# A softcap attention with two gated MLPs on one core: x's high part written by a second product from PSUM

## The chip, the cores and the metric

The kernel runs on one core of a Trainium2 chip. The metric is the device time of one execution in microseconds; the time before is the median of three runs. A profile of one further execution shows what each engine did: PE is TensorE (PEld its weight loads), DVE is VectorE, ACT is ScalarE, POOL is GpSimd and SP is SyncE, which issues most of the DMAs.

## The reference

The reference does attention with softcapped scores, then two MLPs, in float32 (cut):

```python
batch, n_heads, seq, head_dim = (4, 12, 448, 64)

scores = scale * np.matmul(q, k.transpose(0, 1, 3, 2))
scores = cap * np.tanh(scores / cap)
scores = scores - np.max(scores, axis=-1, keepdims=True)
attn = np.exp(scores)
attn = attn / (np.sum(attn, axis=-1, keepdims=True) + 1e-09)
x = np.matmul(attn, v)                     # then (B * S, H * D)

gate = 1.0 / (1.0 + np.exp(-(x @ w_gate)))  # d_ff 1536
x = gate * (x @ w_val) @ w_out
h = x @ w_in                               # d_ff 2048
return (h * np.cos(h)) @ w_out2
```

## The kernel before

The batch of four is done in two halves of two images. A half goes through attention, and its MLP follows. Attention works on pairs of heads: a half has 12 pairs (two images by six pairs of heads), so there are 24 in all. The transposed layout puts the two heads of a pair on the 128 partitions (64 each) and the 448 positions on the free axis.

The products need more than the rounded type of the fast matmul (fp32r), so an operand is kept as two parts: a high part, which is the value rounded to fp32r, and a low part, which is the value less the high part. For attention's result these are `x[:, 0]` and `x[:, 1]`, in a tile x of two images for each pair of heads. The first MLP reads them as its moving operands.

`attention(hf)` is a generator, and each `yield` ends a quarter of a step. In step i, with quarters c from 0 to 3, the work of several pairs stands side by side:

- `a_scores` of pair i: six matmuls into PSUM (L391) and a tanh on ACT (L394) in each quarter.
- `a_exp` (L400): exp on ACT over half of a pair's scores, and behind it on POOL the sum of the two blocks (L404). The first sum of pair i falls in c = 2, the second, which adds to it, in c = 0 of the next step.
- `a_sum` (L408, c = 2): DVE adds the last block to the sum of pair i - 1.
- `a_prep` (c = 0 and 2): PE transposes q, then k, of pair i + 2 into PSUM (t, L370); DVE rounds them (L374) and subtracts (L375) into st.
- `a_norm` of pair i - 2 (c = 0): two matmuls with ones make the denominators (den, L436); DVE takes the reciprocal (L439) and multiplies p.v by it (L440).
- `a_pv` of pair i - 1 (c = 2): 16 matmul passes into pv (L420).
- `a_split` of pair i - 2 (c = 2): DVE copies the product into x's high part (L448), and POOL subtracts it for the low part (L449). For the last pair of a half, DVE does the subtraction too.

The order in the code is the order on each engine (`tc.manual_schedule()`), each engine works through its queue in that order, and the waits are semaphores that follow from the data and from buffers that come free. The tiles t, pv and den share four PSUM buffers, the big tiles (st, p, x, g and others) share 18 SBUF buffers.

Beside attention of the first half runs the preparation of the first weight units: ACT takes absolute value and sign (L156, L158), DVE does four integer steps (L163, L165, L169, L173), then ACT rounds (L236) and POOL subtracts (L237). Three units are done in pieces between the quarters of the first stage. The second half's attention has no such pieces. In what follows the first attention stage is that of the first half, up to some 125 us, and the second one that of the second half, most of which stands at 390 to 485 us.

Of the kernel before, what the change touches and what calls it, by code (L numbers as in the profile page):

```python
# [8 lines left out]
F32R = mybir.dt.float32r  # L9
I32 = mybir.dt.int32  # L10
AF = mybir.ActivationFunctionType
ALU = mybir.AluOpType
PSUM = bass.MemoryType.PSUM

P = 128
# [12 lines left out]
def softcap_attention_gated_mlp_cos_mlp(  # L28
# [18 lines left out]
    nc = tc.nc  # L47
    B, H, S, D = q.shape
# [6 lines left out]
    BH = 2  # L55
# [39 lines left out]
    def big_tile(shape, dtype, name):  # L95
        return big.tile(shape, dtype, tag="big", name=name)
# [242 lines left out]
    x_t = {}  # L339
# [92 lines left out]
    def a_norm(b, hp):  # L432
        s = s_t.pop((b, hp))
        den = psA.tile([P, 512], F32, tag="A", name=f"den{b}_{hp}")
        for h in range(2):
            nc.tensor.matmul(den[h * D : (h + 1) * D, :S], lhsT=ones[:CP], rhs=s[:CP, h, :], start=True, stop=True)  # L436
        pv = pv_t.pop((b, hp))
        r = tmp.tile([P, 2, S], F32, tag="tmp", name=f"r{b}_{hp}")
        nc.vector.reciprocal(out=r[:, 0], in_=den[:, :S])  # L439
        nc.vector.tensor_tensor(out=r[:, 1], in0=pv[:, :S], in1=r[:, 0], op=ALU.mult)  # L440
        r_t[b, hp] = r

    def a_split(b, hp, engine):
        r = r_t.pop((b, hp))
        if b % BH == 0:
            x_t[hp] = big_tile([P, 2, BH, S], F32R, f"x{b}_{hp}")
        x = x_t[hp]
        nc.vector.tensor_copy(out=x[:, 0, b % BH], in_=r[:, 1])  # L448
        engine.tensor_tensor(  # L449
            out=x[:, 1, b % BH], in0=r[:, 1], in1=x[:, 0, b % BH].bitcast(F32), op=ALU.subtract  # L450
        )

    def attention(hf):
# [16 lines left out]
        for i in range(n + 1):  # L470
            if i + 3 < n:
                a_load(*mine[i + 3])
            for c in range(NC):
                if i + 1 < n and c == 3:
                    a_load_v(*mine[i + 1])
                if i < n:
                    a_scores(*mine[i], c)
                if i and c == 0:
                    a_exp(*mine[i - 1], 1)
                if i < n and c == 2:  # L480
                    a_exp(*mine[i], 0)
                if i and c == 2:
                    a_sum(*mine[i - 1])
                if i + 2 < n and c % 2 == 0:
                    a_prep(*mine[i + 2], c // 2)
                if 1 < i < n and c == NORM:
                    a_norm(*mine[i - 2])
                if i:
                    for cc in PVS[c]:
                        a_pv(*mine[i - 1], cc)  # L490
                if 1 < i < n and c == SPLIT:
                    a_split(*mine[i - 2], nc.gpsimd)
                if i >= n - 1 and c == 3:
                    a_norm(*mine[i - 1])
                if i == n and c == 0:
                    a_split(*mine[i - 2], nc.gpsimd)
                if hf == 0 and (i, c) in UNIT_LOADS:
                    w_load()
                if hf == 0 and (i, c) in UNIT_PIECES:
                    next(pieces, None)  # L500
                yield
        if hf == 0:
            for _ in pieces:
                pass
        a_split(*mine[n - 1], nc.vector)


# [270 lines left out]
```

## Time and profile before

| | |
|---|---|
| median of three runs | 1229.07 us (1226.44 to 1229.52) |
| profiled execution | 1222.13 us |
| its span, first to last instruction | 1220.3 us |
| PE busy | 1198.6 us, 98% |
| DVE busy | 685.8 us, 56% |
| ACT busy | 592.3 us, 49% |
| POOL busy | 443.3 us, 36% |
| DVE's copy into x (L448) | 24 times, 21.3 us in all |
| DVE's product (L440) | 24 times, 15.0 us in all |

Busy time is the sum of an engine's instructions, and it is an average over stages with different limits; the shares of a stage are read from the windows. An instruction that is held inside the engine counts as busy for as long as it is held. The chain of work that ended last tells which engine the end of the run depended on at each moment.

### The profile page before, as it was taken

The numbers are of one execution on the slowest core, as the hardware profiler recorded it, in microseconds if no ns is written. First come the engines' busy times: TensorE is split into PE (matmuls) and PEld (weight loads), VectorE is DVE, ScalarE is ACT, GpSimd is POOL, SyncE is SP. The second block draws the span as 40 slices with busy tenths as digits, with TensorE's granted clock in tenths as the row PEclk, the third lists the DMA queues.
The fourth block names the chain that finished last, engine by engine and source line by source line (L and its number), as shares of the span: only waits on it lengthen the run. The fifth ranks groups of instructions, "written<-read, shape, count | busy, mean of one in ns | idle before, by whom it ended". The sixth has DMA issues, their size and how long they took to land.

```text
span 1220.3 us, 15888 instructions
## 1 busy us (share of the span) xinstructions
PE 1198.6 (98%) x6342; PEld 1033.8 (85%) x6342; DVE 685.8 (56%) x729; ACT 592.3 (49%) x664; POOL 443.3 (36%) x234
## 2 busy tenths in 40 slices
PE   8989999999999999999999999999999999999998
PEld 4445889999987456999999998899999999999998
DVE  6998688778732997557566475501414434024242
ACT  6886455445426885444544345533515345344250
POOL 2767123233314675222233223432514333335140
PEclk9999999999999999999999999999999999999999
DMA  6431465555833340365655674221211631213003
GB/s 156 127 96 59 159 220 166 166 171 161 230 131 109 83 134 1 96 209 198 208 174 190 212 238 145 65 66 33 82 42 33 203 102 52 66 33 99 18 27 98
DMA packets 127082, 148.17 MB, mean 121 GB/s; under 512 B 50080, under 2 KB 100640, under 8 KB 127008
## 3 DMA queue, kind: packets, MB, share of 16 engines
q1 hardware_dynamic: 126720, 147.09, 39.4%
q8 instruction: 50, 0.82, 0.3%
q14 instruction: 24, 0.20, 0.0%
q10 hardware_dynamic: 288, 0.07, 0.0%
HBM read 112.13 MB, written 35.00 MB: 121 GB/s over the span
## 4 chain that ended last, share of the span: by engine, by line
PE 74%; DVE 13%; DMA 5%; ACT 4%; issue 3%; SPq 1%; POOL 0%; DVEq 0%; ACTq 0%; POOLq 0%
PE po L633 17%; PE ph L512 16%; PE pv L512 12%; PE pg L512 11%; PE py L512 7%; PE pv L420 4%; PE s L391 3%; DMA wz_raw<-in_moe_w_out_dram 2%; DVE r L439 2%; PE more L633 1%; DMA wi_raw<-in_moe_w_in_dram 1%; PE t L370 1%; DVE f L169 1%; DVE fb L169 1%; PE den L436 1%
## 5 line engine op out<-in xcount | busy, mean ns | idle before, releaser
L237 POOL TENSOR_TENSOR w<-f,w 128x768 fp32r<-128x768 f32 (+1 forms) x140 | 267.3, 1915 | 666.1 <-ACT w L236 570.2
L633 PE MATMUL po<-w,z 128*128 128x384 f32 x1248 | 220.8, 334 | 2.3 <-POOL w L237 2.3
L633 PEld LDWEIGHTS po<-w,z 128*128 128x128 f32 x1248 | 216.7, 188 | 3.2 <-POOL w L237 2.9
L512 PE MATMUL pv<-x,w 128*128 128x448 f32 x864 | 180.0, 366 | 1.0 <-DVE sg L561 1.0
L512 PE MATMUL pg<-x,w 128*128 128x448 f32 x864 | 179.8, 366 | 0.0
L512 PE MATMUL py<-g,w 128*128 128x448 f32 x864 | 177.5, 366 | 0.0
L512 PEld LDWEIGHTS pv<-x,w 128*128 128x128 f32 x864 | 162.0, 188 | 16.0 <-issue 3.1
L512 PEld LDWEIGHTS pg<-x,w 128*128 128x128 f32 x864 | 162.0, 188 | 14.6 <-issue 0.7
L512 PEld LDWEIGHTS py<-g,w 128*128 128x128 f32 x864 | 161.6, 188 | 13.7 <-issue 1.0
L236 ACT CAST w<-f 128x768 fp32r<-128x768 f32 (+1 forms) x140 | 112.1, 808 | 40.5 <-DVE f L173 16.2
L680 DVE TENSOR_SCALAR n<-u 128x896 f32<-128x896 f32 (+1 forms) x38 | 25.1, 660 | 186.6 <-ACT u L679 186.6
L512 PE MATMUL ph<-y,w 128*128 128x448 f32 x576 | 120.8, 371 | 2.3 <-ACT y L585 1.9
L512 PEld LDWEIGHTS ph<-y,w 128*128 128x128 f32 x576 | 109.2, 190 | 13.3 <-ACT y L585 2.2
L512 PE MATMUL ph<-ya,w 128*128 128x448 f32 x576 | 119.5, 368 | 0.0
L512 PEld LDWEIGHTS ph<-ya,w 128*128 128x128 f32 x576 | 108.1, 188 | 10.8
L394 ACT ACTIVATE p<-s,tanh_scale 112x896 f32<-112x896 f32 x96 | 93.1, 1011 | 42.6 <-PE s L391 42.5
L400 ACT ACTIVATE p<-p,cap_sb 112x1792 f32<-112x1792 f32 x48 | 86.3, 1799 | 0.1
L391 PEld LDWEIGHTS s<-st 64*112 64x112 f32 x576 | 45.7, 171 | 41.1 <-ACT p L394 19.0
L420 PE MATMUL pv<-p,v 112*64 112x448 f32 x384 | 77.5, 545 | 2.7 <-PE t L370 2.7
L439 DVE RECIPROCAL r<-den 128x448 f32<-128x448 f32 x24 | 70.8, 2950 | 8.6 <-PE den L436 8.6
L391 PE MATMUL s<-st 64*112 64x448 f32 x576 | 73.5, 381 | 1.6 <-ACT p L394 1.4
L404 POOL TENSOR_TENSOR sum<-p 112x896 f32<-112x896 f32 x24 | 55.8, 2327 | 48.7 <-ACT p L400 23.8
(82 smaller groups left out, 1206.3 us busy)
## 6 DMA issues: line engine op xcount, KB each, us to landing
f<-kept SPq DMA_DIRECT2D x96, 384.0 KB, 3.1
kept<-f SPq DMA_DIRECT2D x36, 384.0 KB, 2.7
wi_raw<-in_moe_w_in_dram SPq DMA_DIRECT2D x16, 768.0 KB, 5.7
kept<-fb SPq DMA_DIRECT2D x30, 384.0 KB, 2.7
wz_raw<-in_moe_w_out_dram SPq DMA_DIRECT2D x14, 768.0 KB, 5.1
wg_raw<-in_moe_w_gate_dram SPq DMA_DIRECT2D x12, 768.0 KB, 5.2
wv_raw<-in_moe_w_val_dram SPq DMA_DIRECT2D x12, 768.0 KB, 4.8
wo_raw<-in_moe_w_out_dram SPq DMA_DIRECT2D x12, 768.0 KB, 4.8
```

Source lines behind the costliest of these rows:

```text
L169: nc.vector.scalar_tensor_tensor(out=gi, in0=lo, scalar=28, in1=gi, op0=ALU.logical_shift_right, op1=ALU.bitwise_or)
L236: nc.scalar.copy(out=t[:, 0], in_=r)
L237: nc.gpsimd.tensor_tensor(out=t[:, 1], in0=r, in1=t[:, 0].bitcast(F32), op=ALU.subtract)
L391: nc.tensor.matmul(ps[:CP, h, :S], lhsT=st[r, ki, ks], rhs=st[r, qi], start=(n == 0), stop=(n == 2))
L394: nc.scalar.activation(out=pt[:CP, j], in_=ps[:CP, :, :S], func=AF.Tanh, scale=tanh_scale[:CP])
L400: nc.scalar.activation(out=pt[:CP], in_=pt[:CP], func=AF.Exp, scale=cap_sb[:CP])
L404: nc.gpsimd.tensor_tensor(out=s, in0=pt[:CP, 1] if half == 0 else s, in1=pt[:CP, 0], op=ALU.add)
L420: nc.tensor.matmul(pv[h * D : (h + 1) * D, :S], lhsT=tv[:, h, c, :], rhs=pt[:CP, j, h, :], start=(c == 0), stop=(c == NC - 1),)
L439: nc.vector.reciprocal(out=r[:, 0], in_=den[:, :S])
L512: nc.tensor.matmul(ps[:, c, :S], lhsT=w[:, wi, kk, :], rhs=x[:, xi, c, :], start=(first and (wi, xi) == (0, 0)), stop=(last and (wi, xi) = ...
L633: nc.tensor.matmul(pos_t[t][:, :NB], lhsT=zf[kk][:, zi, t * P : (t + 1) * P], rhs=ws[kk // UK][:, wi, kk % UK, :], start=(kk == 0 and (zi, ...
L680: nc.vector.tensor_scalar_add(out=n[:, c], in0=u[:, c], scalar1=ROUND)
```

## The change

The high part of x is no longer a copy of the finished product in SBUF. `a_norm` computes the product of pv and the reciprocal a second time, and this second product reads PSUM again and writes x's high part, rounded to fp32r. The first product, in float32, still goes to `r[:, 1]`; the subtraction for the low part reads both as before. The x tile is now allocated in `a_norm`, two quarters earlier.

```diff
         nc.vector.reciprocal(out=r[:, 0], in_=den[:, :S])
         nc.vector.tensor_tensor(out=r[:, 1], in0=pv[:, :S], in1=r[:, 0], op=ALU.mult)
+        if b % BH == 0:
+            x_t[hp] = big_tile([P, 2, BH, S], F32R, f"x{b}_{hp}")
+        nc.vector.tensor_tensor(out=x_t[hp][:, 0, b % BH], in0=pv[:, :S], in1=r[:, 0], op=ALU.mult)
         r_t[b, hp] = r
 
     def a_split(b, hp, engine):
         r = r_t.pop((b, hp))
-        if b % BH == 0:
-            x_t[hp] = big_tile([P, 2, BH, S], F32R, f"x{b}_{hp}")
         x = x_t[hp]
-        nc.vector.tensor_copy(out=x[:, 0, b % BH], in_=r[:, 1])
         engine.tensor_tensor(
```

On DVE the instruction moves. The place is the second step in which the first stage normalizes a pair (pair 1, the reciprocal at 33.73 us of the trace), with weight pieces between; r, pv and den are the tiles of that pair, st and t those of later pairs, f is a weight unit. Before:

```order
L439 RECIPROCAL r_1_476<-den_1_473 128x448
L440 TENSOR_TENSOR r_1_476<-pv_1_425,r_1_476 128x448
L163 TENSOR_SCALAR f_403<-f_403 128x768
L408 SCALAR_TENSOR_TENSOR sum_2_415<-sum_2_415,guard,p_2_1_405 112x896
L374 CAST st_5_465<-t_0_5_503 128x448
L375 TENSOR_TENSOR st_5_465<-t_0_5_503,st_5_465 128x448
L448 CAST x_1_519<-r_1_476 128x448
L165 TENSOR_SCALAR f_403<-f_403 128x768
```

Now:

```order
L439 RECIPROCAL r_1_476<-den_1_473 128x448
L440 TENSOR_TENSOR r_1_476<-pv_1_427,r_1_476 128x448
L443 TENSOR_TENSOR x_1_479<-pv_1_427,r_1_476 128x448
L163 TENSOR_SCALAR f_405<-f_405 128x768
L408 SCALAR_TENSOR_TENSOR sum_2_417<-sum_2_417,guard,p_2_1_407 112x896
L374 CAST st_5_465<-t_0_5_505 128x448
L375 TENSOR_TENSOR st_5_465<-t_0_5_505,st_5_465 128x448
L165 TENSOR_SCALAR f_405<-f_405 128x768
```

The write of x's high part moved ahead of L163 and L408, and L165 now follows directly on L375. In the next step (pair 2, the reciprocal at 42.66 us) another weight operation, L169, stands between the product and L408. Before:

```order
L440 TENSOR_TENSOR r_2_561<-pv_2_510,r_2_561 128x448
L169 SCALAR_TENSOR_TENSOR f_403<-wg_raw,f_403 128x768
L408 SCALAR_TENSOR_TENSOR sum_3_500<-sum_3_500,guard,p_3_1_490 112x896
L374 CAST st_0_550<-t_1_0_586 128x448
L375 TENSOR_TENSOR st_0_550<-t_1_0_586,st_0_550 128x448
L448 CAST x_2_602<-r_2_561 128x448
```

Now:

```order
L440 TENSOR_TENSOR r_2_561<-pv_2_512,r_2_561 128x448
L443 TENSOR_TENSOR x_2_564<-pv_2_512,r_2_561 128x448
L169 SCALAR_TENSOR_TENSOR f_405<-wg_raw,f_405 128x768
L408 SCALAR_TENSOR_TENSOR sum_3_502<-sum_3_502,guard,p_3_1_492 112x896
L374 CAST st_0_550<-t_1_0_588 128x448
L375 TENSOR_TENSOR st_0_550<-t_1_0_588,st_0_550 128x448
```

Here the new product stands ahead of L169 and L408. The orders of PE, ACT, POOL and SP are unchanged; on POOL the subtraction L449 still stands between the two sums L404.

## Rows read from the trace of the kernel before

**Rows 1.** Windows: stretch, its length, then busy time (and instructions) by engine

```profile
23.00:89.00 66.00, 59.45 (x386) 30.29 (x386) 64.96 (x67) 57.41 (x52) 43.06 (x23) 1.00 0.43 114
390.00:458.00 68.00, 68.00 (x446) 33.80 (x442) 63.35 (x65) 59.25 (x51) 44.74 (x24) 1.00 0.43 116
```

**Rows 2.** Waits of PE, 23 to 125 us: us in total, times, longest

```profile
PE den L436 <- DVE sum L408: 5.5, 5, 1.7
PE pv L420 <- PE t L370: 2.7, 4, 0.9
```

**Rows 3.** Chain that ended last, 10 to 135 us: start, us, what

```profile
30.53 2.10 DVE x L448
...
40.06 1.02 DVE x L448
...
46.27 2.35 DVE f L169
...
50.87 0.30 DVE x L448
...
59.01 1.03 DVE x L448
...
67.00 1.68 DVE x L448
...
73.86 1.93 DVE f L165
...
78.05 0.30 DVE x L448
```

**Rows 4.** Single lines: duration in ns as shortest/median/longest

```profile
L448 DVE CAST x<-r x24: 377/1104/2179, 30.4 to 484.4; 128x448 fp32r<-128x448 f32 x24
...
L440 DVE TENSOR_TENSOR r<-pv,r x24: 624/625/627, 27.6 to 483.7; 128x448 f32<-128x448 f32 x24
...
L375 DVE TENSOR_TENSOR st<-t,st x48: 624/624/626, 6.9 to 457.2; 128x448 fp32r<-128x448 f32 x48
```

**Rows 5.** Timeline, 22 to 50 us: start, us, engine, line, tiles, form

```profile
27.63 0.62 DVE L440 TENSOR_TENSOR r<-pv,r 128x448 f32<-128x448 f32 x1
...
28.18 1.15 DVE L408 SCALAR_TENSOR_TENSOR sum<-sum,guard,p 112x896 f32<-112x896 f32 x1
...
30.27 2.11 POOL L404 TENSOR_TENSOR sum<-p 112x896 f32<-112x896 f32 x1 [2.12 <-ACT p L400]
...
30.44 2.18 DVE L448 CAST x<-r 128x448 fp32r<-128x448 f32 x1
```

**Rows 6.** Timeline of POOL and of DVE, 383 to 390 us

```profile
384.10 4.50 POOL L237 TENSOR_TENSOR w<-f,w 128x768 fp32r<-128x768 f32 x2
...
384.17 2.72 DVE L408 SCALAR_TENSOR_TENSOR sum<-sum,guard,p 112x896 f32<-112x896 f32 x1 [3.17 <-POOL sum L404]
```

**Rows 7.** Timeline, 22 to 72 us, third and fourth step

```profile
45.68 2.12 POOL L404 TENSOR_TENSOR sum<-p 112x896 f32<-112x896 f32 x1 [1.07 <-issue]
...
54.07 1.78 ACT L400 ACTIVATE p<-p,cap_sb 112x1792 f32<-112x1792 f32 x1
...
56.67 1.14 DVE L408 SCALAR_TENSOR_TENSOR sum<-sum,guard,p 112x896 f32<-112x896 f32 x1
...
56.82 2.96 POOL L404 TENSOR_TENSOR sum<-p 112x896 f32<-112x896 f32 x1
...
58.43 0.97 PE L436 MATMUL den<-sum,ones 112*64 112x448 f32 x4
```

**Rows 8.** Timeline, end of the second stage

```profile
484.83 0.62 DVE L449 TENSOR_TENSOR x<-r,x 128x448 fp32r<-128x448 f32 x1
...
485.60 2.59 PE L512 MATMUL pg<-x,w 128*128 128x448 f32 x12
```

**Rows 9.** Timeline, inside the second stage

```profile
415.46 1.14 DVE L408 SCALAR_TENSOR_TENSOR sum<-sum,guard,p 112x896 f32<-112x896 f32 x1
...
416.37 2.21 POOL L404 TENSOR_TENSOR sum<-p 112x896 f32<-112x896 f32 x1 [1.36 <-issue]
```

## The prediction, as put down before the changed kernel was run

> **What bounds the kernel now.** I read the windows by stage first, then the waits of TensorE (PE), then the chain that ended last, then the timeline around the copy that goes. In the second attention stage PE is busy 68.00 of 68.00 us [rows 1]: nothing that VectorE (DVE) saves there can shorten the run. In the first stage, 23 to 89 us, it is the other way round: DVE is busy 64.96 of 66.00 us and PE 59.45 [rows 1]. PE's waits say for whom: 5.5 us for the sum of L408 and 2.7 us at pv [rows 2], where the matmul needs a bank that DVE's last read of t frees. Those 8.2 us are the most that any relief of DVE can give back. The chain of that stretch runs along DVE, and the copy that the change removes, L448, is on it six times [rows 3]. It is of one form each time and yet takes from 0.38 to 2.18 us [rows 4]. The timeline shows why: the copy at 30.44 starts while POOL's sum of 30.27 runs, and ends at 32.62, 0.24 us after that sum [rows 5]. So a copy in SBUF that meets a running POOL instruction waits for its end. The operations that convert weights show the same hold: L169 and L165 cost the chain 2.35 and 1.93 us at 46.27 and 73.86 [rows 3], and L408 at 384.17 took 2.72 us [rows 6] against 1.15 at 28.18 [rows 5]. The product L440, which reads PSUM and one operand in SBUF, never shows it: 624 to 627 ns in all 24 [rows 4].
>
> **The change, part by part.** *Removed:* the six copies on the chain, 2.10 + 1.02 + 0.30 + 1.03 + 1.68 + 0.30 = 6.43 us [rows 3]. The six later copies of this stage are not on the chain; I take nothing for them. *Added:* a second product of L440's form, right behind the first. L440 starts at 27.63 and L408 at 28.18 [rows 5], so it costs the chain 0.55 us; six make 3.30 us. Gross gain 6.43 - 3.30 = 3.1 us, if nothing else moves.
>
> Something else does: the holds do not belong to the copy. POOL's first sum of a pair starts when ACT's exp is done, whatever DVE does, and DVE's next operation that can be held meets it. Step by step, by pairs. Step 1 loses its 2.10 us copy, but PE runs without a gap there, so DVE only gains lead. In step 2 the copy's 1.02 us goes, and L165 right behind it now takes the rest of the hold; I keep 0.4 us. In step 3 the product stands ahead of L169, which was waiting for POOL anyway: the sum of 45.68 ends at 47.80 [rows 7] whatever DVE does, and L169 ends 0.8 us behind it, at 48.6 as before. That L169 absorbs the 0.55 us of the product, but also the 0.4 us won before; 0.3 us come back from the copy behind it. Step 6 (L165, 1.93 us [rows 3]) and step 7 (L173) are alike. In step 5 the hold of the fifth copy passes to L163 behind it, which leaves 0.2 us of its 1.68.
>
> Step 4 is where the change may lose. There L408 began at 56.67, just ahead of POOL's first sum at 56.82, which therefore took 2.96 us, not 2.11 as at 30.27 [rows 5, 7]. Exp ends at 54.07 + 1.78 = 55.85 [rows 7], and POOL's queue will be free by then, since its subtraction for x no longer waits for a late copy. L408 comes at 56.67 + 0.55 - 0.3 = 56.9 and finds the sum running until about 58.06. It then ends at 59.2 in place of 57.81, and den, which PE took up at 58.43 [rows 7], waits 0.8 us. Step 5 has no such loss and wins it back.
>
> What is left where PE takes over, at 89 us, is the little that steps 6 and 7 win behind their weight operations: **net gain 0.3 us**. As bounds I take 0.8 us lost (step 4 not won back) and 3.1 us won (no hold moves). The value lies near the lower end because three of the seven steps have a held weight operation that sets the time by POOL's end.
>
> *Moved and at no cost:* POOL's subtraction for x gets its input earlier (for the first pair at 28.8 in place of 32.62 [rows 5]) and stays behind the first sum in POOL's queue. Could it take its turn before a waiting DVE operation? At 384.17 L408 waited for the first of two POOL products and ran before the second (both took 4.50 us, so the second was pushed back) [rows 6]; I take it that DVE goes first. If not, a weight operation is held once more, a loss of the slower rival's kind. PSUM: pv is read 0.55 us longer; no wait row of PE names L440, so 0, and at most 0.55 us per pair if its bank were wanted at once. SBUF: x takes its buffer of 18 one allocation earlier; no DMA or queue of SP is moved. Second stage: PE covers it all. If that cover were gone, a pair's step on DVE would still be shorter, by the 1.1 us of the median copy [rows 4] less 0.55. At its end the last product is 0.62 us, the copy 0.40: x's low part would be ready 0.1 to 0.2 us later than 485.45, but PE's block of 485.60 [rows 8] first does six matmuls, about 1.2 us, on another x. So 0.
>
> **The rivals.** *Relief reaches PE.* For it: DVE's 98% in 23 to 89 us; against it: the holds that stay. It gives the gross 3.1 us, up to the 8.2 us of PE's waits: 1226.0 us, at the very best 1220.9.
>
> *L408 falls behind POOL's first sum in step after step* (slower). The product delays L408 by 0.55 us, POOL starts when exp ends, and whoever is later waits out the other. The point from which it decides is L408 starting after the sum. In the first stage that costs about 0.8 us of PE in step 4; if six of the seven steps met it and none was won back, 6 x 0.8 = 4.8 us, 1233.9 us. In the second stage L408 now leads by 0.91 us (415.46 against 416.37 [rows 9]); the product takes 0.55 of that, while the copy's absence lets the reciprocal start earlier, so it should stay ahead. Against the rival: weight operations hold DVE in only some steps, and a step without them is shorter than before. The Trainium skill (SBUF — State Buffer, "Who interferes with whom") says the port that DVE and GpSimd share is locked by whoever issues first, for the whole instruction, and that a DVE instruction with two SBUF inputs needs it. By that L408 can lose to the sum, as here; the trace agrees (2.72 us at 384.17).
>
> *The copy was the cheaper instruction* (slower, a little). A copy that nothing holds takes 0.38 us and the product 0.62 [rows 4]. If all holds stayed with the operations behind, each pair would pay 0.24 to 0.25 us more: 24 x 0.245 = 5.9 us of DVE, of which the six on the chain make 1.5 us: 1230.6 us. The Trainium skill (VectorE: DVE Perf Modes, "Mode 2×_2P — use both read ports for one tensor") has the rule behind this: a copy from SBUF to SBUF moves two elements a cycle, an operation with two tensors or a PSUM input one. The trace agrees with it for the shortest copies, and not for the median of 1.10 us, which a hold makes.
>
> *The change does nothing of the kind*: the product might take longer than L440 since it writes x's rounded type. L375 has the same types from PSUM at 624 to 626 ns [rows 4], so I give it little; at 1 us each it would cost 2.7 us on the chain.
>
> **How the numbers follow.** The profiled execution took 1222.13 us, span 1220.3; the median of the runs shown is 1229.07 (1226.44 to 1229.52), 0.6% above it. I carry the change over in microseconds: 1221.8 on the profile's scale, 1228.8 on the median's. Chances: forecast 0.62; relief 0.20; L408 behind 0.09; dearer product 0.07; nothing of the kind 0.02. About 0.3% (3.7 us) is what a measurement of this kernel can tell from no change. Faster by more needs the upper half of the relief, 0.10, plus the spread of the runs, 0.04: 0.14. Slower by more is most of the slower rival plus a little of the others: 0.08. Within: 0.78. The range, 1225.0 to 1231.5, takes in the forecast with the runs' spread of 3.1 us, the dearer product and the relief at 3.1 us; it leaves out the large relief and the worst of L408, under 0.2 together.
>
> **What would show it.** Right: no L448, 24 more products at 0.62 us; L169, L165 and L173 of the first stage end as late as before, with longer holds on L163 and L165; L408 near 57 us held by a sum; PE's wait at den still 5 us or more in 23 to 125 us; the second stage at 68 of 68 us. Wrong: den's wait falls to 3 us or less and the stage's end comes 2 us or more earlier (relief); L408 held in most steps (slower); product longer than 0.63 us.

## The result, and the profile after

The changed kernel took 1235.59 us (median of 6 runs, 1233.49 to 1239.51), the kernel before beside it 1229.30 (6 runs, 1225.02 to 1231.25): ratio 1.0071, interval 1.0052 to 1.0090. It is 6.3 us slower; the forecast was 1228.8 with a range up to 1231.5.

The profiled execution took 1233.49 us, its span 1231.7. By stage (stretch, its length, then busy time of PE, PEld, DVE, ACT and POOL, granted clock, DMA share, GB/s; first and last row answer to [rows 1]):

```profile
23.00:89.00 66.00, 59.57 (x364) 29.68 (x361) 64.68 (x62) 53.11 (x48) 41.30 (x22) 0.92 0.39 101
89.00:125.00 36.00, 31.76 (x180) 16.16 (x178) 32.34 (x28) 26.93 (x24) 26.00 (x15) 0.95 0.12 35
390.00:458.00 68.00, 68.00 (x439) 35.37 (x438) 57.25 (x61) 56.66 (x50) 45.88 (x25) 1.00 0.36 93
```

The second stage is as foreseen: DVE is relieved (57.25 in place of 63.35 us), PE is busy 68.00 of 68.00 us, and nothing comes of it. In the first stage PE's busy time has hardly moved (59.57 against 59.45), but with fewer matmuls in it (364 against 386) and at a granted clock of 0.92, where the row of before has 1.00. PE's waits of 23 to 125 us (us in total, times, longest), to be read beside [rows 2]:

```profile
PE den L436 <- DVE sum L408: 9.4, 5, 3.1
PE pv L420 <- PE t L370: 0.6, 1, 0.6
```

The wait for t has gone from 2.7 to 0.6, in part by DVE's relief (0.41 us at 42.84 is gone, 0.92 at 70.44 is 0.63). The other two, 0.69 each at 53.33 and 80.51, stand right behind den groups that came late, so PE itself came later there. The wait for L408 has grown by more, 5.5 to 9.4. The product itself is what was forecast, a little less (count, then shortest, median and longest in ns, beside [rows 4]):

```profile
L443 DVE TENSOR_TENSOR x<-pv,r x24: 614/614/616, 28.1 to 491.5; 128x448 fp32r<-128x448 f32 x24
```

**Where the time went** is read by taking the same group of matmuls in both traces and subtracting its start before from its start after. Before the loss begins PE is 0.58 us ahead (pv at 42.26 against 42.84). Then it falls behind in three bites: den at 50.51 against 49.73 is 0.78 late, and t behind it 2.67; den at 80.37 against 76.91 is 3.46 late; den at 92.42 against 86.45 is 5.97 late, and pv behind it 7.1. From there to 490 us little moves: den at 116.59 against 109.43 is 7.16 late. The first bite, in the timeline of the changed kernel, 44 to 62 us (start, us, engine, line, what, and in brackets the idle time ahead of it and its releaser):

```profile
45.40 0.61 DVE L443 TENSOR_TENSOR x<-pv,r 128x448 fp32r<-128x448 f32 x1
45.58 2.12 POOL L404 TENSOR_TENSOR sum<-p 112x896 f32<-112x896 f32 x1 [1.36 <-issue]
45.93 2.58 DVE L169 SCALAR_TENSOR_TENSOR f<-wg_raw,f 128x768 int32<-128x768 int32 x1
47.66 1.84 POOL L449 TENSOR_TENSOR x<-r,x 128x448 fp32r<-128x448 f32 x1
48.44 2.02 DVE L408 SCALAR_TENSOR_TENSOR sum<-sum,guard,p 112x896 f32<-112x896 f32 x1
50.51 1.76 PE L436 MATMUL den<-sum,ones 112*64 112x448 f32 x4 [3.09 <-DVE sum L408]
52.20 2.58 PE L391 MATMUL s<-st 64*112 64x448 f32 x12
...
58.15 2.10 POOL L404 TENSOR_TENSOR sum<-p 112x896 f32<-112x896 f32 x1 [0.82 <-POOL w L237]
58.37 2.83 DVE L408 SCALAR_TENSOR_TENSOR sum<-sum,guard,p 112x896 f32<-112x896 f32 x1
```

and the same place in the kernel before, with the den group of 109.43:

```profile
48.53 1.14 DVE L408 SCALAR_TENSOR_TENSOR sum<-sum,guard,p 112x896 f32<-112x896 f32 x1
49.73 0.97 PE L436 MATMUL den<-sum,ones 112*64 112x448 f32 x4 [1.72 <-DVE sum L408]
50.63 1.48 PE L391 MATMUL s<-st 64*112 64x448 f32 x12
51.25 1.78 POOL L449 TENSOR_TENSOR x<-r,x 128x448 fp32r<-128x448 f32 x1 [3.45 <-DVE x L448]
...
109.43 0.97 PE L436 MATMUL den<-sum,ones 112*64 112x448 f32 x4 [1.43 <-DVE sum L408]
```

Read the POOL rows. Before, L449 waited 3.45 us for the copy and ran long after L408. After, its input is written at 46.01 and it stands directly behind the sum. L169 had lain waiting since 45.93 and goes when the sum ends at 47.70, as forecast; L449, issued at 47.66, waits for L169 (1.84 us, where an undisturbed one takes 1.13). But when L169 ends, the waiting L449 goes before L408, which is next on DVE. L408 takes 2.02 us in place of 1.14, and den comes late. Then look at PE's own rows: the same den takes 1.76 in place of 0.97 us and s 2.58 in place of 1.48. The windows around the three waits (same columns as above) say why:

```profile
49.41:56.23 6.82, 5.72 (x22) 2.90 (x24) 6.75 (x7) 3.02 (x4) 3.16 (x3) 0.50 0.28 91
80.12:83.53 3.41, 3.16 (x12) 1.56 (x14) 3.38 (x5) 0.27 (x1) 2.08 (x1) 0.50 0.00 0
93.79:97.20 3.41, 3.41 (x16) 1.90 (x15) 3.38 (x3) 3.41 (x4) 2.38 (x2) 0.50 0.34 113
```

The granted clock was 0.50 there, the 1.2 GHz level. It fell within den's waits of 3.09 and 2.47 us, and 1.4 us behind the one of 2.53; the kernel before stood at 1.00, the 2.4 GHz level, in all of 23 to 125 us. The second bite is the first again, with L165 at 76.59, L449 at 77.91 and L408 held to 2.02 us at 78.29. The third is different: here POOL went twice running.

```profile
87.28 2.12 POOL L404 TENSOR_TENSOR sum<-p 112x896 f32<-112x896 f32 x1 [4.67 <-issue]
88.59 2.71 DVE L173 SCALAR_TENSOR_TENSOR f<-f,wv_raw 128x768 int32<-128x768 int32 x1
89.35 1.13 POOL L449 TENSOR_TENSOR x<-r,x 128x448 fp32r<-128x448 f32 x1
91.22 1.14 DVE L408 SCALAR_TENSOR_TENSOR sum<-sum,guard,p 112x896 f32<-112x896 f32 x1
92.42 0.97 PE L436 MATMUL den<-sum,ones 112*64 112x448 f32 x4 [2.53 <-DVE sum L408]
```

L173 waits out the sum and L449 too (2.71 us; 0.95 when free), and pushes L408 back.

**The working theory** (turn): L449, ready early, gets the port that both engines read through ahead of L408 or of the weight operation in front of it; PE's wait grows; and the half clock behind a long wait adds to it. The rivals are two: the 0.5 us of the product alone pushes L408 into POOL's sums (called position below), or the product is simply the dearer instruction, 0.61 us against 0.38 of a free copy (called dearer product).

### The profile page after: what moved, and what is told of

It is laid out like the page before. It is cut to its first block, busy times and chain, and to the rows that moved or that the text cites. A ratio compares the mean times of both kernels' runs of the same rounds, so it can differ in the third digit from the quotient of the medians.

```text
span 1231.7 us, 15887 instructions
## 1 busy us (share of the span) xinstructions
PE 1205.8 (98%) x6342; PEld 1034.9 (84%) x6342; DVE 690.6 (56%) x729; ACT 592.5 (48%) x664; POOL 442.6 (36%) x234
## 4 chain that ended last, share of the span: by engine, by line
PE 71%; DVE 14%; DMA 6%; ACT 5%; issue 3%; POOL 1%; SPq 1%; DVEq 0%; ACTq 0%; POOLq 0%
PE po L633 17%; PE ph L512 16%; PE pv L512 11%; PE pg L512 10%; PE py L512 7%; PE pv L420 4%; PE s L391 3%; DMA wz_raw<-in_moe_w_out_dram 2%; DMA wi_raw<-in_moe_w_in_dram 2%; DVE r L439 2%; DVE fb L163 1%; PE t L370 1%; PE more L633 1%; DVE fb L173 1%; DVE f L169 1%
## 5 line engine op out<-in xcount | busy, mean ns | idle before, releaser
L237 POOL TENSOR_TENSOR w<-f,w 128x768 fp32r<-128x768 f32 (+1 forms) x140 | 269.1, 1928 | 676.3 <-ACT w L236 591.7
L404 POOL TENSOR_TENSOR sum<-p 112x896 f32<-112x896 f32 x24 | 53.9, 2244 | 56.4 <-issue 25.3
```

Of the source, the lines that this page charges most:

```text
L237: nc.gpsimd.tensor_tensor(out=t[:, 1], in0=r, in1=t[:, 0].bitcast(F32), op=ALU.subtract)
L404: nc.gpsimd.tensor_tensor(out=s, in0=pt[:CP, 1] if half == 0 else s, in1=pt[:CP, 0], op=ALU.add)
```

## The experiments

The table gives, for every kernel run, how far PE is behind the first trace of the kernel before (us; median of up to five groups of matmuls from the mark on; the marks are times in that trace), and the ratio of times with its interval.

| kernel | 42 | 58 | 76 | 90 | 125 | ratio |
|---|---|---|---|---|---|---|
| changed kernel | -0.58 | 2.61 | 4.21 | 7.30 | 7.16 | 1.0071 (1.0052 to 1.0090) |
| after_again | -0.62 | 2.95 | 4.63 | 6.14 | 5.96 | 1.0063 (1.0039 to 1.0088) |
| before_again | 0.17 | 0.17 | 0.17 | 0.18 | 0.16 | 1.0021 (0.9997 to 1.0044) |
| only_pair_2 | 0.14 | 3.29 | 3.28 | 3.29 | 3.26 | 1.0012 (0.9995 to 1.0029) |
| not_2_5_6 | -0.59 | 0.38 | 0.38 | 0.41 | 0.06 | 1.0002 (0.9984 to 1.0019) |
| pair_2_low_late | 0.12 | 1.65 | 1.59 | 1.58 | 1.55 | one run |
| low_late_2_5_6 | -0.23 | 2.61 | 2.10 | 1.92 | 1.72 | 1.0025 (0.9998 to 1.0052) |
| low_behind_second_sum | 0.49 | 2.06 | 1.71 | 1.52 | 6.71 | 1.0058 (1.0031 to 1.0086) |
| only_pair_2_fill | -0.11 | 1.46 | 1.35 | 1.36 | 1.19 | one run |
| after_fill | -0.53 | 2.41 | 2.86 | 4.41 | 4.21 | 1.0044 (1.0017 to 1.0071) |
| not_2_5_6_fill | -0.46 | 0.96 | 0.44 | 0.47 | -0.01 | 1.0002 (0.9975 to 1.0029) |
| copy_at_norm | -0.41 | 3.05 | 5.63 | 6.74 | 11.78 | 1.0088 (1.0061 to 1.0114) |
| product_at_split | 0.64 | 0.95 | 1.98 | 4.59 | 4.82 | 1.0054 (1.0033 to 1.0076) |
| extra_product | 2.53 | 2.93 | 3.38 | 5.60 | 6.71 | 1.0160 (1.0137 to 1.0182) |
| sum_early_after | 0.88 | 4.07 | 3.47 | 6.52 | 8.71 | 1.0093 (1.0062 to 1.0124) |
| sum_early_before | 1.36 | 0.70 | -0.68 | 1.26 | 1.27 | 1.0023 (1.0005 to 1.0041) |
| pieces_late_after | 1.01 | 5.86 | 3.48 | 6.36 | 6.84 | 1.0055 (1.0035 to 1.0076) |

### What belongs to the change: both kernels once more

> The changed kernel once more, nothing altered. Theory turn (POOL's subtraction L449, now ready early and lying right behind POOL's first sum, takes the port that both engines read through between DVE's weight operation and L408; the end of L408 then comes late, PE waits for it with the den matmuls, and its granted clock halves behind the long waits): L408 is held by L449 again in the first attention stage (2.0 us in place of 1.14, at two or three of its steps), PE waits 8 to 10 us for L408 between 23 and 125 us, three stretches at half clock stand there, and PE is 6 to 8 us behind the kernel before at 125 us. Theory late part (the some 3 us that were lost between 490 and 560 us come with the execution and not with the change): PE loses under 1 us there this time. If they come with the change, 2.5 to 3.5 us again. Time 1233 to 1239.

> The kernel before once more, nothing altered, for a second trace of it. The profiled execution shown of it took 1222.13 us, under all of its other runs (1224.4 to 1231.3), and all four traces taken since lose 2.2 us against it between 490 and 600 us and about 1 us near 750 us. Theory late part (that comes with the execution): the new trace loses those 3 us too, from 490 us on, and is level with the first to within 1 us at 125 us; time 1226 to 1230. If the late part comes with the change, the new trace stays level from 490 to 600 us.

The two profiled executions of the changed kernel are 11.4 and 9.8 us longer than the first one of the kernel before. The second trace of the kernel before is level with the first up to 125 us (0.16), with the same waits for L408, and then loses 3.6 us by 490 and in all 13.5 us by the end, with nothing changed: its span was 1233.8. So differences behind 125 us come with the execution; the first trace of before was simply a quick one. The first 125 us repeat to some 0.2 us in the kernel before and to 1.2 in the changed one, and its delay there, 6.0 to 7.2 us, is as large as the 6.3 us by which the medians differ. It also repeats its rows: L408 takes 2.02 us at 48.40 and 2.01 at 78.66. One difference is the clock: the half stretch near 94 us was missing, and the third bite (76 to 90 us) is 1.5 us in place of 3.1. before_again's ratio shows what a timing here can't tell from 1.

### Which steps: the product for some pairs only

The two kernels are the kernel before with the second product for the pairs named, and the copy at its old place for the rest; x's tile is allocated in `a_norm` for all, as in the changed kernel. The diff is that of only_pair_2; not_2_5_6 has the condition `pairs.index((b, hp)) not in (2, 5, 6)`.

```diff
+        if pairs.index((b, hp)) == 2:
+            nc.vector.tensor_tensor(out=x_t[hp][:, 0, b % BH], in0=pv[:, :S], in1=r[:, 0], op=ALU.mult)
...
-        nc.vector.tensor_copy(out=x[:, 0, b % BH], in_=r[:, 1])
+        if not (pairs.index((b, hp)) == 2):
+            nc.vector.tensor_copy(out=x[:, 0, b % BH], in_=r[:, 1])
```

> The second product for one pair alone: the third of the 24 (index 2), whose reciprocal stands at 42 to 45 us. All others keep the copy at the old place. Up to 125 us two executions of the kernel before lay within 0.2 us of each other, so one step can be read from the trace. Theory turn: L449 of this pair runs right behind POOL's first sum, L408 takes 2.0 in place of 1.14, PE waits 3 us for it, half clock follows, and PE is 2 to 3.2 us behind the kernel before from 52 to 60 us; whatever of that DVE's later slack takes back, 1 to 3 us stay at 125 us: time 1229 to 1232. Theory sum of small delays (only all products together push L408 back): behind by 0.6 us at 52 us and by less than 1 at 125 us; 1227 to 1230.

> The second product for all pairs but three (indices 2, 5 and 6, at whose steps at 48, 78 and 88 us the changed kernel lost its time); these three keep the copy at the old place. Theory turn with its three steps: PE is within 1 us of the kernel before at 90 us, no half clock up to 90 us, at most 1.5 us behind at 125 us; time 1226 to 1230. Theory position (the place of the loss depends on where L408 stands against POOL's sums, and moves on): it turns up at other steps, 2 us or more at 90 us or 3 at 125 us, 1231 to 1235.

One product in 24 costs 3.3 us, and none of it is won back by 125 us: 3.29 at 58 us, 3.26 at 125. The other nine of the first stage together leave PE where it was (0.06 us; the kernel before repeated itself to 0.16). So the loss lies at the three steps, of which only that of pair 2 was tried by itself, and DVE's relief elsewhere (0.59 us at 42) comes to nothing by 125. not_2_5_6 also speaks against the dearer product: nine of the first stage's twelve products stand there in place of copies and cost nothing by 125 us. Against its expectation the clock halved at 49.41 us there too, with no product at that step: L169 went ahead of the first sum, which then held L408 to 2.98 us at 46.25. By the times only_pair_2 is 1.5 us slower, with an interval that includes the 3.3 us and none. In its timeline the first bite has the form of the third, since L169 comes 0.9 us later here:

```profile
45.80 2.12 POOL L404 TENSOR_TENSOR sum<-p 112x896 f32<-112x896 f32 x1 [1.06 <-issue]
46.85 2.97 DVE L169 SCALAR_TENSOR_TENSOR f<-wg_raw,f 128x768 int32<-128x768 int32 x1
47.88 1.13 POOL L452 TENSOR_TENSOR x<-r,x 128x448 fp32r<-128x448 f32 x1
49.74 1.14 DVE L408 SCALAR_TENSOR_TENSOR sum<-sum,guard,p 112x896 f32<-112x896 f32 x1
50.94 1.76 PE L436 MATMUL den<-sum,ones 112*64 112x448 f32 x4 [2.78 <-DVE sum L408]
52.63 2.58 PE L391 MATMUL s<-st 64*112 64x448 f32 x12
```

(The subtraction is L452 here.) The expectation's number, 2 to 3.2 us at 52 to 60, was met to 0.1 us; its detail, L408 itself held to 2.0 us, was not: L169 was.

### L449 out of the way

L449 is written behind POOL's second sum, one step later. So that no buffer is held longer, the first product then writes straight into the low part's place in the matmuls' type, which makes the low part zero.

```diff
-        nc.vector.tensor_tensor(out=r[:, 1], in0=pv[:, :S], in1=r[:, 0], op=ALU.mult)
+        low = x_t[hp][:, 1, b % BH] if pairs.index((b, hp)) in LATE else r[:, 1]
+        nc.vector.tensor_tensor(out=low, in0=pv[:, :S], in1=r[:, 0], op=ALU.mult)
...
-                if 1 < i < n and c == SPLIT:
+                if 1 < i < n and c == SPLIT and not (hf == 0 and i - 2 in LATE):
                     a_split(*mine[i - 2], nc.gpsimd)
...
                     a_exp(*mine[i], 0)
+                if hf == 0 and c == 0 and i - 3 in LATE:
+                    a_split(*mine[i - 3], nc.gpsimd)
```

This is low_late_2_5_6 (LATE = 2, 5, 6, on the changed kernel); pair_2_low_late does it for pair 2 on only_pair_2, low_behind_second_sum for all pairs of both stages.

> As the one before, and L449 of this one pair behind POOL's second sum instead of behind the first, written in place (the low part of this pair is zero by it). Theory turn: L408 takes 1.14 at 48 us, PE waits 1.5 to 2.2 us for it, no half clock near 50 us, PE is 0 to 0.7 us behind the kernel before from 52 to 60 us. Theory position: L408 starts 0.5 us later whatever L449 does, and PE is 1.5 us or more behind.

> The changed kernel with L449 of the three pairs 2, 5 and 6 written behind POOL's second sum, as in the run for one pair (their low part is zero by it, its time the same). Theory turn: L408 takes 1.14 at 48 and 78 us and the weight operation at 88 us is held by the sum alone (1.7 in place of 2.7); what stays is half clock at 50 us (1.0 to 1.6 us) and little else, so PE is 1 to 3 us behind at 125 us; time 1228 to 1232. Theory position (0.5 us later is enough without L449): 5 us or more behind at 125 us, 1233 to 1237.

> The changed kernel with L449 written behind POOL's second sum (one step later) in place of behind the first, so that it can't lie ready beside L408. To have no buffer held longer for it, the first product is written straight into the place of the low part, in the type of the matmuls, and L449 works in place: the low part is thereby zero, and its time the same. Theory turn: L408 takes 1.14 at the steps of some 48 and 78 us, PE waits 4 to 6.5 us for it in all, and the time is 1227 to 1231. Theory position alone (the product pushes L408 back until it meets POOL's next first sum, as at 58 us): that loss stays, one or two steps of 1 to 2 us each with their half clock behind them, 1230 to 1234. Theory dearer product: 1233 to 1237.

pair_2_low_late is the sharpest of these. Its timeline:

```profile
46.83 1.91 DVE L169 SCALAR_TENSOR_TENSOR f<-wg_raw,f 128x768 int32<-128x768 int32 x1
48.67 1.14 DVE L408 SCALAR_TENSOR_TENSOR sum<-sum,guard,p 112x896 f32<-112x896 f32 x1
49.86 1.35 PE L436 MATMUL den<-sum,ones 112*64 112x448 f32 x4 [1.75 <-DVE sum L408]
51.14 2.58 PE L391 MATMUL s<-st 64*112 64x448 f32 x12
```

The product is there, L449 is not: L169 absorbs the product's 0.55 us, L408 starts 0.14 us later than in the kernel before (48.67 against 48.53) and den 0.13. Theory position has lost for this step. Yet s takes 2.58 us, and PE is 1.6 us behind, which I had put at 0 to 0.7: the half clock came behind a wait of 1.75 us, after 1.72 had left it at full level in both traces of the kernel before.

With all three steps mended, 1.72 us of the 6.0 to 7.2 are left at 125 us. L408 took 1.14 us at the first two steps, and the third weight operation 1.23 in place of 2.71 (low_late_2_5_6, whose line numbers are one higher, so that L408 is L409 here and L173 is L174):

```profile
48.78 1.14 DVE L409 SCALAR_TENSOR_TENSOR sum<-sum,guard,p 112x896 f32<-112x896 f32 x1
...
61.27 0.97 PE L437 MATMUL den<-sum,ones 112*64 112x448 f32 x4 [1.50 <-DVE sum L409]
...
77.81 1.14 DVE L409 SCALAR_TENSOR_TENSOR sum<-sum,guard,p 112x896 f32<-112x896 f32 x1
...
86.17 1.23 DVE L174 SCALAR_TENSOR_TENSOR f<-f,wv_raw 128x768 int32<-128x768 int32 x1
```

**The turn, with the clock behind it, is 4.2 to 5.4 us of the loss.** This run has every product of the changed kernel, so the dearer product can have at most the rest, and half clock at 50 us and the prediction's step 4 (den at 61.27, of which more below) account for most of the 2.61 us at 58.

Moving L449 everywhere left PE 1.52 us behind at 90 us. L408 was clean at 48.79 and 86.93, but at 75.57 the first sum held it to 3.00 us, at no cost to PE (1.7 us behind ahead of it and after). Between 90 and 125 us it lost 5.2 us: there L408 was held at 102.09, 110.60 and 120.34 (2.04, 2.96 and 2.05 us), by L449 at its new place or by a sum, and the clock halved at 112 us. That expectation (1227 to 1231) missed; neither of L449's two places is clear of DVE in all steps.

### The clock by itself: matmuls of no use in the waits

In front of the den matmuls that wait, four more into the same bank (two in not_2_5_6_fill), overwritten by the true ones. The orders of DVE and POOL are left as they were.

```diff
+    FILL = {3: 4, 6: 4, 7: 4}
...
         den = psA.tile([P, 512], F32, tag="A", name=f"den{b}_{hp}")
+        k = pairs.index((b, hp))
+        for q in range(FILL.get(k, 0)):
+            pt = p_t[pairs[k + 1][0], pairs[k + 1][1], 0]
+            nc.tensor.matmul(
+                den[q % 2 * D : (q % 2 + 1) * D, :S], lhsT=ones[:CP], rhs=pt[:CP, 0, q % 2, :], start=True, stop=True
+            )
```

> The kernel with the second product for the third pair alone, and the same four matmuls of no use in front of the den matmuls that wait 2.8 us for L408 there. Theory clock: no half clock at 50 us, PE is 1.0 to 1.4 us behind from 52 to 125 us (L408's late end alone: den came 1.2 us later in that kernel) in place of 3.3. If the clock has no part: 3.0 to 3.6.

> The changed kernel with four matmuls of no use (2 x 448 columns twice, about 1.9 us by the den row of 0.97) in front of the den matmuls of three pairs, into the same bank, which the true ones then overwrite: PE works while it waits for L408 at the steps of 50, 80 and 92 us, where it waited 3.1, 2.5 and 2.5 us. DVE and POOL do the same as in the changed kernel. Theory clock (the half clock behind long waits is a loss of its own, about 3.9 of the 7.2 us at 125 us; the late L408 is the other 4.3): no half clock near 50, 80 and 93 us, and PE is 3 to 4.5 us behind the kernel before at 125 us instead of 6 to 7.2; time 1230 to 1233. If the late L408 is all: 6 to 8 us behind, 1234 to 1238.

> The kernel with the second product for all pairs but 2, 5 and 6, which was level with the kernel before at 125 us, having been 0.6 us ahead up to 47 us and lost 1.0 at a stretch of half clock at 49 us behind a wait of 1.9 us; two matmuls of no use (1.0 us) fill that wait. Theory clock: it stays 0.3 to 0.7 us ahead up to 125 us, and its time is 1225 to 1229, which no timing here can tell from the kernel before. If the clock has no part: level or behind at 125 us.

The first stage of after_fill, and its first bite:

```profile
23.00:89.00 66.00, 59.46 (x382) 29.42 (x381) 64.69 (x63) 53.80 (x48) 42.66 (x23) 1.00 0.38 100
```

```profile
47.41 1.72 PE L440 MATMUL den<-p,ones 112*64 112x448 f32 x8
50.55 0.97 PE L444 MATMUL den<-sum,ones 112*64 112x448 f32 x4 [1.43 <-DVE sum L408]
51.46 1.47 PE L391 MATMUL s<-st 64*112 64x448 f32 x12
...
58.44 2.57 DVE L408 SCALAR_TENSOR_TENSOR sum<-sum,guard,p 112x896 f32<-112x896 f32 x1
...
61.07 0.97 PE L444 MATMUL den<-sum,ones 112*64 112x448 f32 x4 [1.35 <-DVE sum L408]
```

L408 is held as before (2.02 us at 48.48), den starts at the same time as in the changed kernel (50.55 against 50.51), but den takes 0.97 and s 1.47 us: the clock stayed at 1.00 through 23 to 125 us. PE is 4.21 us behind at 125 instead of 5.96 and 7.16, and 1.19 instead of 3.26 where only pair 2 has the product (1.36 instead of 3.29 at 90). **The clock's share is 1.8 to 3.0 us**, less than the 3.9 I had expected, and 1.9 to 2.1 us of a single step's 3.3. One reason is in the last two rows. At 57.73 PE was 1.24 us late in place of 2.59, but then the first sum held L408 of 58.44, den waited 1.35 us, and PE was 2.4 us late again. So what the clock costs at the first bite hides what the next hold would cost, and the two can't be added. The third bite also took another form: L173 ran free at 88.06 (0.95 us), and L449 held L408 behind it (2.03 us at 88.93). The time, 1234.90, missed the 1230 to 1233 expected. By the times, 1.0044, it can't be told from the changed kernel, whose interval overlaps; the trace's 4.21 us would be 1.0034. not_2_5_6_fill missed in part: it stayed 0.3 us ahead past 52 us, but at 56.88 L408 then met a first sum that had begun at 56.49 (2.67 us), and the lead was gone by 58.

### The operation without the place, the place without the operation

```diff
# copy_at_norm, against the changed kernel
-        nc.vector.tensor_tensor(out=x_t[hp][:, 0, b % BH], in0=pv[:, :S], in1=r[:, 0], op=ALU.mult)
+        nc.vector.tensor_copy(out=x_t[hp][:, 0, b % BH], in_=r[:, 1])
# product_at_split, against the kernel before, in a_split
-        nc.vector.tensor_copy(out=x[:, 0, b % BH], in_=r[:, 1])
+        nc.vector.tensor_tensor(out=x[:, 0, b % BH], in0=pv[:, :S], in1=r[:, 0], op=ALU.mult)
# extra_product, against the kernel before, in a_norm
         nc.vector.tensor_tensor(out=r[:, 1], in0=pv[:, :S], in1=r[:, 0], op=ALU.mult)
+        nc.vector.tensor_tensor(out=r[:, 1], in0=pv[:, :S], in1=r[:, 0], op=ALU.mult)
```

> The copy from SBUF as in the kernel before, but written where the second product stands now, right behind the first product. Position without the product. Theory turn: L449 has its input as early as in the changed kernel and takes its turn ahead of L408, so L408 is held again at the steps of some 48 and 78 us, PE's waits for L408 are 8 us or more, and the time is 1232 to 1238. Theory dearer product (0.61 us of a product against 0.38 of a free copy, six times, on DVE's path): without the product there is nothing to lose, and the time is 1228 to 1230.

> The second product, but at the old place of the copy (behind L408 and one cast and product of L374 and L375). The operation without the position. A bank of PSUM is held longer by this, which may cost up to 0.5 us at a step. Theory turn: L449 gets its input some 4 us later, as in the kernel before, POOL stands idle when L408 starts, L408 takes 1.14 again at nearly all steps, PE waits 4 to 6.5 us for it, no half clock between 23 and 125 us, and the time is 1226 to 1231. Theory dearer product: 1232 to 1237, as in the changed kernel.

> The kernel before with its first product written twice, the copy from SBUF kept at its old place behind L408: the delay of the changed kernel (0.5 to 0.6 us in front of the weight operation and L408) without the early input of L449, and with the copy not taken away. The result is the same. Theory turn (L449 being ready early is what costs): L408 is not held by L449 in the first stage; the kernel loses what DVE's added work costs, up to 6 x 0.54 = 3.2 us, and not more: 1229 to 1232. Theory position (0.5 us later is enough for L408 to meet POOL's next sum, with PE's long waits and its clock halving behind them): L408 held by POOL's sums at 2 or more steps, PE's waits for it 8 us or more, half clock between 23 and 125 us, and 1233 to 1238.

copy_at_norm is slower than the product, 11.78 us behind at 125. L449 holds L408 at 48.84, 78.93 and 91.32 (2.02 us each) as in the changed kernel, with no product there, so the place by which L449 is released costs by itself. The run does not tell which instruction is dearer. The copy takes 0.39 us in the median, but at the three steps the first sum held it to 2.03 to 2.16 us, in place of the weight operation:

```profile
45.89 2.15 DVE L443 CAST x<-r 128x448 fp32r<-128x448 f32 x1
47.97 0.94 DVE L169 SCALAR_TENSOR_TENSOR f<-wg_raw,f 128x768 int32<-128x768 int32 x1
48.12 1.78 POOL L449 TENSOR_TENSOR x<-r,x 128x448 fp32r<-128x448 f32 x1 [0.33 <-DVE x L443]
48.84 2.02 DVE L408 SCALAR_TENSOR_TENSOR sum<-sum,guard,p 112x896 f32<-112x896 f32 x1
```

Against the dearer product stand not_2_5_6 and low_late_2_5_6.

product_at_split does not clear the old place: 4.82 us behind, outside what I expected of theory turn (1226 to 1231; it took 1233.6). L408 is clean (1.18 us and less), but another wait has come:

```profile
PE den L436 <- DVE st L375: 8.9, 5, 2.9
PE den L436 <- DVE sum L408: 1.5, 1, 1.5
```

The profile shows that den now waits for L375. My reading is that the late product holds pv's bank of PSUM longer, and that den then gets one of the four banks that L375 of a t frees last; the rotation itself was not traced. I had put this at 0.5 us a step, and because of it this run tells nothing on the turn.

extra_product (the delay, with L449 late and the copy kept) shows theory position at work where nothing absorbs it: L408 meets a first sum and is held to 2.5 to 3.1 us at 38.56, 58.99, 68.32, 96.69 and 105.82, and 6.71 us are lost at 125. Then it loses some 9.5 us more before 490: in the second stage L408 is behind the first sum in step after step (415.19, 424.98, 433.61 and so on, 1.85 to 3.04 us), where it led by 0.91 us before [rows 9].

```profile
L408 DVE SCALAR_TENSOR_TENSOR sum<-sum,guard,p x24: 1139/1854/3069, 21.0 to 492.5; 112x896 f32<-112x896 f32 x24
```

The median of L408 is 1854 ns here; it is 1144 in the changed kernel. At 18.6 us by the medians this is more than either theory had said (up to 1238), since I had not thought of the second stage. It has the copy and one product more, so it tells what a delay can do, not what the change does.

### Other orders

```diff
# sum_early_after and sum_early_before: L408 of the pair behind, right behind the reciprocal
         nc.vector.reciprocal(out=r[:, 0], in_=den[:, :S])
+        if then:
+            a_sum(*then)
# pieces_late_after
-    UNIT_PIECES = [(i, c) for i in range(2, BH * NP) for c in (1, 3)]
+    UNIT_PIECES = [(i, c) for i in range(2, BH * NP) for c in (2, 3)]
```

> The changed kernel with L408 written right behind the reciprocal, ahead of both products and of the weight operation; everything else stays. POOL's second sum, that L408 needs, ended at 44.2, 52.4 and so on, 0.6 to 2 us before the reciprocal's end, and POOL's next first sum starts 0.7 us or more behind that end. Theories turn and position alike say that the loss is L408's late end: with L408 1.1 to 3.6 us earlier it takes 1.14 at most steps, PE waits under 3 us for it between 23 and 125 us, no half clock stands there, PE is level with the kernel before or up to 4 us ahead at 125 us, and the time is 1224 to 1230. Theory dearer product (DVE's added work is the loss, wherever it stands): 1232 to 1237.

> The kernel before with the same move of L408 to right behind the reciprocal; the copy stays where it was, behind the weight operation. It tells what the move is worth by itself, and so whether the second product is a gain once L408 stands in front of it. If the product then gains its 0.5 us a step, this kernel is 1 to 3 us slower than the changed kernel with the move; theory dearer product: this one is quicker than it by 3 us or more. Time 1225 to 1231.

> The changed kernel with the first of the two weight operations of a step written one place later (c = 2 in place of 1), behind L408, so that nothing but the two products stands between the reciprocal and L408. Theory turn: at the steps of some 48 and 78 us it is now L408 that waits for POOL's first sum and goes as its turn comes, with L449 behind it and the weight operation behind that: L408 ends 0.5 to 1.5 us earlier than in the changed kernel, PE waits 4 to 6.5 us for it, and the time is 1227 to 1232. Theory dearer product: nothing changes, 1233 to 1237. If L408 meets the first sums in more steps than before, 1234 or more.

The time of sum_early_before lay where it was expected (1228.8), as slow as the kernel before or slower; the two with the product missed, pieces_late_after by little (1232.25 against 1232 at most). They all shorten the wait at den (2.9 us and 0.8 for L445 in sum_early_after, 1.1 and 0.2 for L442 in sum_early_before, 2.5 in pieces_late_after, counted to 130 us), and PE then waits at pv: 7.1, 4.7 and 6.6 us. The profile names no releaser, but all nine of these waits end some 0.1 us after an L375, which reads t from PSUM, and so do the waits for t in the kernel before (at 42.84, L375 ends at 42.74). So DVE sets pv, and the hold has only changed the instruction that pays. In sum_early_after:

```profile
51.63 2.80 DVE L173 SCALAR_TENSOR_TENSOR f<-f,wg_raw 128x768 int32<-128x768 int32 x1
...
55.00 0.62 DVE L375 TENSOR_TENSOR st<-t,st 128x448 fp32r<-128x448 f32 x1
...
55.72 1.76 PE L420 MATMUL pv<-p,v 112*64 112x448 f32 x4 [3.12 <-issue]
```

In sum_early_before L173 takes 0.95 us at 51.79, and pv waits 1.55. That sum_early_after is 9 us slower than sum_early_before would by itself speak for theory dearer product, but these rows are holds: L173 above by POOL's second sum, and L165 at 78.92 (2.51 us) by a first sum and L449 behind it. No order tried here beats the kernel before; not_2_5_6 is level with it.

## Why the prediction was wrong, point by point

- **What bounds the kernel: right.** First stage by DVE, second by PE at 68.00 of 68.00 us; the product at 0.61 us as costed (0.62); L408 of the second stage free (median 1144 ns).
- **"DVE goes first": the step that failed.** The prediction had one row for it, 384.17, of a DVE instruction that had lain waiting through nearly a whole POOL instruction [rows 6]. It made of that a rule, which fails in two ways. Between two DVE instructions POOL's waiting one goes in: L449 between L169 and L408 at 48.44, between L165 and L408 at 78.29. And a DVE instruction that has waited only a short while loses to the next of POOL: L173 at 88.59, 0.8 us before the sum's end. The Trainium skill (SBUF — State Buffer, "Who interferes with whom") has a lock for the whole instruction, which goes to whoever issues first. The traces agree with the lock (2.02 us at 48.44 for 1.14) and with the order at that step, where L449 was issued at 47.66, but not at the third, where L173 of 88.59 came behind L449 of 89.35. Which of the two goes next is what the prediction had to settle from the rows, and settled wrongly. "A weight operation is held once more" was written down as the loss if so, and given no place and no price: at three of seven steps it would have been 1.13 us for L449 each, 3.4 us, against a net gain of 0.3.
- **Step 3, right but for L449.** "L169 absorbs the 0.55 us" is shown by pair_2_low_late: L408 at 48.67 against 48.53.
- **Step 4, right in kind, too small in size.** L408 at 58.37 met the sum of 58.15 and was held to 2.83 us. In the changed kernel PE was then already 2.6 us late for other reasons, and is hardly later behind it (2.84 at den, 2.61 at pv). Where PE came in time, the same hold cost 1.6 us (low_late_2_5_6), 1.4 (after_fill) and 1.5 (not_2_5_6_fill), against the 0.8 forecast.
- **The clock: a term that was missing.** No row of before showed a half clock in the stage, so the prediction priced late microseconds one for one. The runs put it at 1.8 to 3.0 of the 6.0 to 7.2 us.
- **"Wins it back": right for step 4, not for the bites.** From the den of step 4 to the pv of 70.44, PE won back 0.6 us in the changed kernel and 0.9 in low_late_2_5_6, in after_fill and in not_2_5_6_fill. Where the later steps have the copy it won back nothing: a step's 3.29 us stood at 3.26 us at 125 (only_pair_2). Three bites of 2 to 3 us are far more than that.
- **The slower rival** was given six steps of 0.8 us and 1233.9 us, near the outcome, at 0.09. Its mechanism, L408 behind POOL's first sum in step after step, did not happen in the changed kernel; it did in extra_product. The loss came at three steps, by POOL's other instruction, at 2 to 3 us each.
- **Size, worked out from rows.** From the starts of den and of what follows in the two traces, L408's late ends make 1.36 + 1.18 + 1.76 = 4.3 us; what PE loses behind them, mostly clock, 1.50 + 0.75 + 1.50 = 3.8; the lead of 0.58 and 0.3 regained by 125 us go off: 7.2. after_fill, which keeps late ends of L408 at the three steps and takes the half clock away, measured 4.21. What part of the second the clock has beyond the 1.8 to 3.0 that the fill gave back isn't settled.

## What to carry to other kernels

When an edit makes the input of an instruction on another engine ready earlier, that instruction is a moved instruction too: list what it will now stand beside, and price it at every step as if it went first. Where two engines share a port, a row that shows who won once is no rule; look for rows in which the loser had waited a short and a long time. And where PE waits in a stage bound by another engine, ask what a microsecond more of idling does to its granted clock before taking a delay at face value.

## What the runs showed of the hardware

**Whose turn it is at the port.** The first 500 us of all 18 traces hold 82 cases of a DVE instruction that took over 0.25 us more than its shortest because of a running POOL instruction, while another one of POOL followed within 0.05 us. Where DVE's had waited 1.08 us or more at the end of the running one it went first, 53 of 53; 18 of these are one place, that of [rows 6], once in each trace. At 0.81 or less POOL went again, 7 of 7. From 0.83 to 1.07 DVE went first in 17 of 22. A case just under the bound speaks against a sharp line: L163 at 36.92 in low_behind_second_sum had waited 0.36 us, lost 0.24, and went first. That is an observation for these pairs of instructions (L408 and the weight operations against L404, L449 and L237); what decides it is not known.

**The clock behind a wait.** At one place in the program, den of about 50 us, PE's wait was 1.72 us in two traces of the kernel before and the clock stayed at the 2.4 GHz level; after 1.75 us in pair_2_low_late, 1.87 in not_2_5_6, 2.20 in low_late_2_5_6 and 2.78 to 3.31 in others it fell to 1.2 GHz, during the wait or behind it. It did not fall behind 1.43 us with matmuls of no use ahead of it, nor behind 2.57 in product_at_split, so the wait alone does not tell it. At other places the same program had it once and once not (93.79 us in the changed kernel, not in after_again). So of two kernels with nearly equal waits one can lose 1.6 us more than the other.

**Spread behind 125 us.** The kernel before, run twice, is level to 0.16 us up to 125 us and 13.5 us apart at the end. A single pair of traces of this program can't be subtracted there.
